# Keys and queries loaded in runs of six tokens, and put in order by products that write their columns six apart

## The chip, the cores and the metric

The kernel runs on one core of one Trainium2 chip. The metric is the device time in microseconds (us) of one execution, and the lower the better. A core has a matrix engine (TensorE, PE in the profile; its loading of weights is the row PEld), VectorE (DVE), ScalarE (ACT), GpSimd (POOL) and SyncE (SP, which here issues all transfers). The matrix engine reads SBUF and writes PSUM.

## The reference, cut to what matters

An attention feeds two mixtures of experts. The attention has 4 batches of 8 heads, 576 tokens and 64 features; it is the sum of a coarse part over the means of four tokens and of a local part over the seven nearest tokens.

```python
q_d = q.reshape(B, H, Sd, factor, D).mean(axis=3)      # factor = 4, Sd = 144; k_d, v_d alike
out_up = np.repeat(sm_attn(q_d, k_d, v_d), factor, axis=2)
mask = np.abs(pos[:, None] - pos[None, :]) < factor
scores = np.where(mask, scale * np.matmul(q, k.transpose(0, 1, 3, 2)), -1000000000.0)
...
x = (out_up + softmax(scores) @ v)                     # as [2304 tokens, 512 features]
x = _moe_ref(x, phi, w1, w2)                           # first mixture, 8 experts of 4 slots
return _moe2_ref(x, w_gate, w1, w2)                    # second mixture, 8 experts of 1024
```

## The kernel before, in words

The attention goes by units: a unit is a pair of heads of one batch, so there are 16 units, four to a batch. Each unit passes through some 35 parts (load, transpose, copy, score, softmax, products, sum), and the table ORDER writes down by hand in which order a step emits its parts and by how many steps each lags behind. A step therefore holds one part of each kind, for different units, and each engine runs its own parts in that order. Four batch parts (lps; lt and lnp; dnp; sip) join in three of each four steps.

The parts that the change touches are these. `load_qk` (L193) asks for keys and queries, one step before they are used. Keys come with tokens 96 i to 96 i + 95 side by side on 96 partitions, one run of 64 features (256 bytes) for each token and head. Queries come in the same way, but for the units in WIDE_Q (0, 2, 3, 9, 12, 13): there each partition takes six tokens that follow each other, one run of 1,536 bytes. `transpose_k` (L238) and `transpose_q` (L262) put the features on the partitions, in PSUM tiles kps and qps: six transposes of 96 columns, or for the queries of WIDE_Q twelve products with the identity, each of a head's 64 features. In the second form token 6 g + i lands at place g of product i, so `copy_q` (L277) puts the tokens in order on its way from PSUM to SBUF:

```python
out=t[:, 0:S].rearrange("p (g a i) -> p a i g", a=2, i=3),
in_=pv.rearrange("p a (i g) -> p a i g", i=3), func=ACTF.Copy,
```

`pool_k` (L247, tile kd) on VectorE and `copy_k` (L253, tile kt) on ScalarE read kps; `copy_q` (tile qt) reads qps; the scores `score_loc` (L313, tile sl) and `score_pool` (L327, tile sd) follow. kps, qps, ptp, loc, lps and lt share two buffers in PSUM (the pool p2, tag t2).

SP issues the transfers in the order of the steps: keys and queries of one unit, weight tiles (wa, 1 MB each) where LOADS asks for some, then the values twice, as windows (vw, runs of 256 bytes) and as groups of four tokens (vg, runs of 1,024 bytes). After the loop SP asks for the other 24 weight tiles. Then comes the first mixture (its first product is tile h at L711) and the second, which takes the larger part of the time and is TensorE's.

Of the kernel before, what the change touches and what calls it, by code (L numbers as in the profile page):

```python
# [18 lines left out]
# A step of the attention, in order of emission: a part, and by how many steps it lags behind the  # L19
# unit's (or, for the parts in BATCH, the batch's) own step.  # L20
# [11 lines left out]
# What the steps leave of the last units and batches, in order of emission.  # L32
# [9 lines left out]
# Weight tiles of the first mixture that are asked for in a step.  # L42
LOADS = {-2: 1, 8: 2, 9: 1, 11: 2, 12: 2, 15: 3}
# Units before this one keep their pooled queries padded with zero rows, the others a head at a time.
PADDED = 2
# Units whose queries come in long runs and are transposed by products with the identity.
WIDE_Q = frozenset((0, 2, 3, 9, 12, 13,))
# [3 lines left out]
def attn_moe_moe_kernel(  # L51
# [13 lines left out]
    nc = tc.nc  # L65
# [39 lines left out]
    def make_masks(m0):  # L105
        # keys 1 .. 7 after the query's place in its block; the first and the last block also
        # lose the keys that pass the ends of the sequence
# [60 lines left out]
    # =================== attention ===================  # L168
    with ExitStack() as actx:
# [19 lines left out]
        def rows(src, b, h, first, ap):  # L189
            s0 = src[b, h]  # L190
            return bass.AP(tensor=s0.tensor, offset=s0.offset + first * D, ap=ap)

        def load_qk(u):  # L193
            b, hp = units[u]
            d = U[u] = {}
            kn = d["kn"] = lq.tile([96, 6, 2, D], FP32, name="kn", tag="kn")
            for h in range(2):
                nc.sync.dma_start(
                    out=kn[:, :, h, :], in_=k[b, 2 * hp + h].rearrange("(i g) d -> g i d", i=6)
                )  # L200
            if u in WIDE_Q:
                qn = d["qn"] = lq.tile([96, 2, 6 * D], FP32, name="qn", tag="qn")
                nc.sync.dma_start(out=qn, in_=rows(q, b, 2 * hp, 0, [[6 * D, 96], [S * D, 2], [1, 6 * D]]))
            else:
                qn = d["qn"] = lq.tile([96, 6, 2, D], FP32, name="qn", tag="qn")
                for h in range(2):
                    nc.sync.dma_start(
                        out=qn[:, :, h, :], in_=q[b, 2 * hp + h].rearrange("(i g) d -> g i d", i=6)
                    )

        def load_v(u):
            # vw: the keys of window t = 4 s + c (24 t - 4 .. 24 t + 28) on partitions 32 c ..;
            # what a window holds past the ends of its sequence has weight zero
# [23 lines left out]
        # q and k with the features of both heads on the partitions  # L237
        def transpose_k(u):  # L238
            d = U[u]
            ps = d["kps"] = p2.tile([128, 2, 512], FP32, name="kps", tag="t2")  # L240
            for i in range(6):
                nc.tensor.transpose(  # L242
                    ps[:, i // 3, 96 * (i % 3):96 * (i % 3) + 96],
                    d["kn"][:, i].rearrange("p h d -> p (h d)"), ident[0:96, 0:96],
                )
# [7 lines left out]
        def copy_k(u):  # L253
            # the keys of a head keep the rows of the other head zero
# [7 lines left out]
        def transpose_q(u):  # L262
            d = U[u]
            qn = d["qn"]
            ps = d["qps"] = p2.tile([128, 2, 512], FP32, name="qps", tag="t2")
            for i in range(6):
                ov = ps[:, i // 3, 96 * (i % 3):96 * (i % 3) + 96]
                if u in WIDE_Q:
                    for h in range(2):
                        nc.tensor.matmul(  # L270
                            out=ov[64 * h:64 * h + 64, :], lhsT=qn[:, h, D * i:D * i + D],
                            rhs=ident[0:96, 0:96], start=True, stop=True,
                        )
                else:
                    nc.tensor.transpose(ov, qn[:, i].rearrange("p h d -> p (h d)"), ident[0:96, 0:96])

        def copy_q(u):  # L277
            t = U[u]["qnt"] = qts[u % 2]
            pv = U[u]["qps"][:, :, 0:288]
            if u in WIDE_Q:  # L280
                # token 6 g + i of a head stands at place g of product i
                nc.scalar.activation(
                    out=t[:, 0:S].rearrange("p (g a i) -> p a i g", a=2, i=3),
                    in_=pv.rearrange("p a (i g) -> p a i g", i=3), func=ACTF.Copy,
                )
            else:
                nc.scalar.activation(out=t[:, 0:S].rearrange("p (a j) -> p a j", a=2), in_=pv, func=ACTF.Copy)

        def pool_q(u):
# [7 lines left out]
            if u < PADDED:  # L297
                # the queries of a head keep the rows of the other head zero
# [191 lines left out]
        # tokens of a batch on the partitions: four tiles, and the last 64 on the upper half  # L490
# [560 lines left out]
```

## Time and profile before

| | |
|---|---|
| Time, median of 3 runs | 1129.81 us (1126.55 to 1130.12) |
| Span of the profiled execution | 1131.3 us; no other time is recorded with it |
| TensorE busy | 1084.3 us, 96% of the span |
| VectorE busy | 523.4 us, 46% |
| ScalarE busy | 361.8 us, 32% |
| First product of the first mixture starts | 171.88 us after the span's start |
| Packets of all transfers | 95,887, 93.41 MB |

The shares are means over the whole span; the attention is only its first 170 us, so it is read from windows of that stretch. Matrix products are pipelined, so that the time of a group of them is better read from its first start to the start of the next group than from its busy time. An fp32 product appears as two instructions (passes), a transpose as one.

### The profile page before, as it was taken

Reading aid. Unit: us, or ns where it says so; the run is one execution under the profiler, and the core shown is the slowest. Engines: PE = TensorE matmul, PEld = TensorE weight load, DVE = VectorE, ACT = ScalarE, POOL = GpSimd, SP = SyncE. Lnnn points to the kernel's source line nnn. Section 1 sums busy time; section 2 is a strip of 40 time slices with the busy share of each in tenths; the row PEclk is TensorE's granted clock in tenths of the full one; section 3 lists DMA queues with packets and bytes.
Section 4 is the critical chain, followed back from the end, with each engine's and each line's share of the span. In section 5 each row is a group of like instructions: output and inputs, shape, how many; then the busy total and the mean of one; then the engine's idle time right before and its main releaser. Section 6 shows DMA issues by size and latency. Waiting matters only on the chain.

```text
span 1131.3 us, 16288 instructions
## 1 busy us (share of the span) xinstructions
PE 1084.3 (96%) x6639; PEld 854.9 (76%) x6639; DVE 523.4 (46%) x1161; ACT 361.8 (32%) x946; POOL 214.5 (19%) x178
## 2 busy tenths in 40 slices
PE   6788877999999999999999999999999999999998
PEld 5666643387888788878887888788788878888886
DVE  5996963165544434344334333434343344334332
ACT  5886741143222322232223222322232222222221
POOL 5654431060049100400040004000400040000000
PEclk9998988889999999999999999999999999999999
DMA  9999998942002200220022002200220010001011
GB/s 193 168 202 214 246 389 313 387 149 75 1 1 75 75 1 1 75 75 1 1 75 75 1 1 75 75 1 1 75 75 1 1 38 1 1 1 38 38 47 47
DMA packets 95887, 93.41 MB, mean 83 GB/s; under 512 B 59076, under 2 KB 64836, under 8 KB 95812
## 3 DMA queue, kind: packets, MB, share of 16 engines
q1 hardware_dynamic: 95812, 92.37, 29.3%
q8 instruction: 52, 0.85, 0.3%
q14 instruction: 23, 0.19, 0.1%
HBM read 87.64 MB, written 4.72 MB: 82 GB/s over the span
## 4 chain that ended last, share of the span: by engine, by line
PE 84%; DVE 1%; ACT 0%; issue 0%; DVEq 0%
PE y L875 71%; PE h L857 6%; PE h L711 1%; PE ap L828 1%; PE so L760 1%; PE as L840 1%; PE sip L610 0%; PE hps L749 0%; DVE c L738 0%; PE cp L734 0%; ACT c L736 0%; PE sp L939 0%; PE sit L691 0%; PE gl L908 0%; ACT aps L832 0%
## 5 line engine op out<-in xcount | busy, mean ns | idle before, releaser
L861 DVE SCALAR_TENSOR_TENSOR hlo<-h,hhi 128x256 fp32r<-128x256 f32 x576 | 243.9, 424 | 499.9 <-ACT hhi L860 498.9
L875 PE MATMUL y<-whi,hlo 128*128 128x512 f32 x1152 | 457.2, 397 | 0.0
L875 PE MATMUL y<-whi,hhi 128*128 128x512 f32 x1152 | 456.9, 397 | 0.0
L875 PE MATMUL y<-wlo,hhi 128*128 128x512 f32 x1152 | 454.6, 395 | 0.0
L860 ACT ACTIVATE hhi<-h 128x256 fp32r<-128x256 f32 x576 | 221.3, 385 | 632.0 <-PE h L857 632.0
L875 PEld LDWEIGHTS y<-whi,hhi 128*128 128x128 f32 x1152 | 216.5, 188 | 57.9 <-ACT aps L832 5.9
L875 PEld LDWEIGHTS y<-wlo,hhi 128*128 128x128 f32 x1152 | 216.8, 188 | 48.5
L875 PEld LDWEIGHTS y<-whi,hlo 128*128 128x128 f32 x1152 | 218.5, 190 | 25.8
L857 PE MATMUL h<-c,a4s 128*128 128x256 f32 x576 | 161.8, 282 | 0.0
L857 PEld LDWEIGHTS h<-c,a4s 128*128 128x128 f32 x576 | 108.9, 189 | 28.5 <-DVE a4s L845 1.7
L810 POOL CAST whi<-w2s 128x2048 fp32r<-128x2048 f32 x14 | 26.5, 1895 | 483.5 <-PE y L875 474.8
L884 DVE SCALAR_TENSOR_TENSOR acc<-y,pg,acc 128x512 f32<-128x512 f32 x126 | 93.7, 743 | 9.9 <-PE y L875 9.7
L811 POOL TENSOR_TENSOR wlo<-w2s,whi 128x2048 fp32r<-128x2048 f32 x14 | 64.7, 4620 | 1.1
L892 POOL TENSOR_SCALAR acc<-acc,pg 128x512 f32<-128x512 f32 x18 | 27.8, 1564 | 79.3 <-DVE pg L949 79.3
L405 DVE STREAM_TRANSPOSE bd<-pl 32x384 f32<-32x384 f32 x64 | 36.4, 569 | 1.9 <-POOL pl L391 0.5
L242 PE MATMUL kps<-ident,kn 96*128 96x96 f32 x96 | 13.1, 282 | 17.5 <-DMA kn<-in_k_dram 9.3
L242 PEld LDWEIGHTS kps<-ident,kn 96*128 96x128 f32 x96 | 10.1, 161 | 21.5 <-issue 9.4
L257 ACT ACTIVATE kt<-kps 64x576 f32<-64x576 f32 x32 | 20.5, 642 | 12.6 <-DVE kd L249 12.4
L391 POOL TENSOR_TENSOR pl<-pl,l 128x384 f32<-128x384 f32 x16 | 13.3, 831 | 57.2 <-DVE l L387 54.5
L400 ACT ACTIVATE pd<-pd,ls 72x144 f32<-72x144 f32 x64 | 21.3, 406 | 8.7 <-DVE ls L386 7.6
L374 ACT ACTIVATE pd<-sd,nm 72x144 f32<-72x144 f32 x64 | 23.1, 372 | 0.1
L464 PE MATMUL loc<-bd,vw 128*64 128x96 f32 x384 | 20.7, 261 | 2.0 <-ACT dT L581 1.6
(169 smaller groups left out, 669.9 us busy)
## 6 DMA issues: line engine op xcount, KB each, us to landing
wa<-in_moe_w_dram SPq DMA_DIRECT2D x32, 1024.0 KB, 7.6
w1s<-in_moe_w_dram SPq DMA_DIRECT2D x16, 1024.0 KB
w2s<-in_moe_w_dram SPq DMA_DIRECT2D x15, 1024.0 KB, 6.9
vw<-in_v_dram SPq DMA_DIRECT2D x62, 96.0 KB, 6.2
kn<-in_k_dram SPq DMA_DIRECT2D x32, 144.0 KB, 6.0
vg<-in_v_dram SPq DMA_DIRECT2D x16, 288.0 KB
out_dram<-acc SPq DMA_DIRECT2D x18, 256.0 KB, 2.0
qn<-in_q_dram SPq DMA_DIRECT2D x20, 144.0 KB, 5.9
```

The lines of the kernel that those rows point to most:

```text
L242: nc.tensor.transpose(ps[:, i // 3, 96 * (i % 3):96 * (i % 3) + 96], d["kn"][:, i].rearrange("p h d -> p (h d)"), ident[0:96, 0:96],)
L374: nc.scalar.activation(out=pd[:, h, a, :], in_=d["sdv"][:, h, a, :], func=ACTF.Exp, scale=scale / 16.0, bias=d["nm"][:, h, a:a + 1], accum ...
L400: nc.scalar.activation(out=d["pd"][:, h, a, :], in_=d["pd"][:, h, a, :], func=ACTF.Copy, scale=ls[:, h, a:a + 1])
L405: nc.vector.transpose(out=bds[u % 2][32 * c:32 * c + 32, :, c, :], in_=U[u]["pl"][32 * c:32 * c + 32])
L810: nc.gpsimd.tensor_copy(out=hi, in_=t)
L811: nc.gpsimd.tensor_tensor(out=lo, in0=t, in1=hi.bitcast(FP32), op=ALU.subtract)
L857: nc.tensor.matmul(out=ps, lhsT=a4s[:, e % 2, 128 * f:128 * f + 128], rhs=c4[:, BLK * b:BLK * b + BLK], start=True, stop=True)
L860: nc.scalar.activation(out=hi[:, f, :], in_=ps, func=ACTF.Relu)
L861: nc.vector.scalar_tensor_tensor(out=lo[:, f, :], in0=ps, scalar=0.0, in1=hi[:, f, :].bitcast(FP32), op0=ALU.max, op1=ALU.subtract)
L875: nc.tensor.matmul(out=ps, lhsT=l[:, f, ts], rhs=r, start=(n == 0), stop=(n == 3 * KF - 1))
L884: nc.vector.scalar_tensor_tensor(out=acc[:, t, :], in0=ps, scalar=pg[:, t, e:e + 1], in1=acc[:, t, :], op0=ALU.mult, op1=ALU.add)
L892: nc.gpsimd.tensor_scalar(out=acc[:, t, :], in0=acc[:, t, :], scalar1=pg[:, t, 0:1], scalar2=None, op0=ALU.mult)
```

## The change

All keys and queries, of every unit, come in the form with six tokens a partition: two transfers for the keys and two for the queries, each of 48 partitions (0 to 47 and 64 to 111, one half of the tokens each) with runs of 1,536 bytes. Both transpositions are made by products with the identity, 24 of them: six token places i, two heads h, two halves a. Each reads 48 partitions, has 64 output partitions and 48 columns, and writes these columns six apart in PSUM, so that token 6 g + i stands at place 6 g + i. `copy_q` has one form left, and WIDE_Q is gone.

```diff
-            kn = d["kn"] = lq.tile([96, 6, 2, D], FP32, name="kn", tag="kn")
-            for h in range(2):
-                nc.sync.dma_start(
-                    out=kn[:, :, h, :], in_=k[b, 2 * hp + h].rearrange("(i g) d -> g i d", i=6)
-                )
...
+            for name, src in (("kn", k), ("qn", q)):
+                t = d[name] = lq.tile([112, 2, 6, D], FP32, name=name, tag=name)
+                for a in range(2):
                     nc.sync.dma_start(
-                        out=qn[:, :, h, :], in_=q[b, 2 * hp + h].rearrange("(i g) d -> g i d", i=6)
+                        out=t[64 * a:64 * a + 48].rearrange("p h i d -> p h (i d)"),
+                        in_=rows(src, b, 2 * hp, 288 * a, [[6 * D, 48], [S * D, 2], [1, 6 * D]]),
                     )
...
+        def transpose(t, ps):
+
+            for i in range(6):
+                for h in range(2):
+                    for a in range(2):
+                        r = slice(64 * a, 64 * a + 48)
+                        nc.tensor.matmul(
+                            out=ps[64 * h:64 * h + 64, a, 0:288].rearrange("p (g i) -> p i g", i=6)[:, i, :],
+                            lhsT=t[r, h, i, :], rhs=ident[r, r], start=True, stop=True,
+                        )
+
         def transpose_k(u):
-            d = U[u]
-            ps = d["kps"] = p2.tile([128, 2, 512], FP32, name="kps", tag="t2")
-            for i in range(6):
-                nc.tensor.transpose(
-                    ps[:, i // 3, 96 * (i % 3):96 * (i % 3) + 96],
-                    d["kn"][:, i].rearrange("p h d -> p (h d)"), ident[0:96, 0:96],
-                )
+            ps = U[u]["kps"] = p2.tile([128, 2, 512], FP32, name="kps", tag="t2")
+            transpose(U[u]["kn"], ps)
...
         def copy_q(u):
             t = U[u]["qnt"] = qts[u % 2]
             pv = U[u]["qps"][:, :, 0:288]
-            if u in WIDE_Q:
...
+            nc.scalar.activation(out=t[:, 0:S].rearrange("p (a j) -> p a j", a=2), in_=pv, func=ACTF.Copy)
```

TensorE's order in a plain step of the loop, before (a row is a group of like instructions, with the output's partitions and columns; numbers behind a name tell buffers apart):

```order
L242 MATMUL kps<-ident,kn 128x96 x6
L445 MATMUL up<-ptd,vd 64x144 x4
L464 MATMUL loc<-bd_120,vw 64x96 x12
L497 MATMUL xn<-ident,xt_116 128x128 x4
L498 MATMUL xh<-ident,xt_116 128x128
L275 MATMUL qps<-ident,qn 128x96 x6
L425 MATMUL ptp<-ident,pd 72x72 x8
L320 MATMUL sl<-kt_110,qt_108 32x64 x24
L333 MATMUL sd<-kd,qd_112 72x144 x4
```

The same step with the change:

```order
L238 MATMUL kps<-ident,kn 64x48 x24
L427 MATMUL up<-ptd,vd 64x144 x4
L446 MATMUL loc<-bd_120,vw 64x96 x12
L479 MATMUL xn<-ident,xt_116 128x128 x4
L480 MATMUL xh<-ident,xt_116 128x128
L238 MATMUL qps<-ident,qn 64x48 x24
L407 MATMUL ptp<-ident,pd 72x72 x8
L302 MATMUL sl<-kt_110,qt_108 32x64 x24
L315 MATMUL sd<-kd,qd_112 72x144 x4
```

The order is the same; six transposes have become 24 smaller products, once for the keys and once for the queries.

SP's order where two steps ask for weights, before (the shape is that of the tile's side; the first qn is of a unit outside WIDE_Q, the second of one inside):

```order
L198 DMA kn<-in_k_dram 96x6x64 x2
L207 DMA qn<-in_q_dram 96x6x64 x2
L162 DMA wa<-in_moe_w_dram 128x2x1024 x2
L221 DMA vw<-in_v_dram 32x12x64 x4
L231 DMA vg<-in_v_dram 72x4x256
L198 DMA kn<-in_k_dram 96x6x64 x2
L203 DMA qn<-in_q_dram 96x2x384
L162 DMA wa<-in_moe_w_dram 128x2x1024
```

And with the change:

```order
L200 DMA kn<-in_k_dram 48x2x384 x2
L200 DMA qn<-in_q_dram 48x2x384 x2
L161 DMA wa<-in_moe_w_dram 128x2x1024 x2
L215 DMA vw<-in_v_dram 32x12x64 x4
L225 DMA vg<-in_v_dram 72x4x256
L200 DMA kn<-in_k_dram 48x2x384 x2
L200 DMA qn<-in_q_dram 48x2x384 x2
L161 DMA wa<-in_moe_w_dram 128x2x1024
```

The queue keeps its order; the runs of kn and qn are 384 elements long instead of 64, and a unit of WIDE_Q has two transfers of qn in place of one.

## Rows read from the trace of the kernel before

**Rows 1.** TensorE's timeline: start, duration, instructions; the first mixture's first product.

```profile
171.88 16.80 PE L711 MATMUL h<-wa,slt 128*32 128x512 f32 x128 [0.44 <-DVE slt L703]
```

**Rows 2.** TensorE's timeline, transpositions of keys; in brackets the idle time before.

```profile
22.74 0.69 PE L242 MATMUL kps<-ident,kn 96*128 96x96 f32 x6 [0.60 <-DMA kn<-in_k_dram]
...
29.20 0.69 PE L242 MATMUL kps<-ident,kn 96*128 96x96 f32 x6 [0.71 <-DMA kn<-in_k_dram]
...
36.60 0.69 PE L242 MATMUL kps<-ident,kn 96*128 96x96 f32 x6 [1.36 <-ACT pd L400]
...
43.90 0.69 PE L242 MATMUL kps<-ident,kn 96*128 96x96 f32 x6 [0.99 <-ACT pd L400]
...
52.52 0.69 PE L242 MATMUL kps<-ident,kn 96*128 96x96 f32 x6 [2.31 <-DMA kn<-in_k_dram]
...
59.56 0.69 PE L242 MATMUL kps<-ident,kn 96*128 96x96 f32 x6 [0.72 <-DMA kn<-in_k_dram]
...
67.82 0.69 PE L242 MATMUL kps<-ident,kn 96*128 96x96 f32 x6 [0.29 <-ACT pd L400]
...
76.34 0.71 PE L242 MATMUL kps<-ident,kn 96*128 96x96 f32 x6
...
85.46 0.71 PE L242 MATMUL kps<-ident,kn 96*128 96x96 f32 x6
...
94.64 0.69 PE L242 MATMUL kps<-ident,kn 96*128 96x96 f32 x6 [2.73 <-DMA kn<-in_k_dram]
...
105.83 1.18 PE L242 MATMUL kps<-ident,kn 96*128 96x96 f32 x6 [2.24 <-DMA kn<-in_k_dram]
...
117.43 0.72 PE L242 MATMUL kps<-ident,kn 96*128 96x96 f32 x6
...
127.01 0.72 PE L242 MATMUL kps<-ident,kn 96*128 96x96 f32 x6
```

**Rows 3.** Windows: stretch, length, each engine's busy time, granted clock, DMA share, GB/s.

```profile
70.00:80.00 10.00, 9.95 (x160) 8.10 (x156) 9.62 (x23) 9.25 (x25) 5.66 (x8) 1.00 1.18 182
100.00:110.00 10.00, 7.76 (x128) 6.10 (x124) 5.31 (x14) 6.29 (x19) 4.65 (x6) 0.79 1.15 183
145.00:150.00 5.00, 3.39 (x52) 2.98 (x51) 4.61 (x16) 2.96 (x11) 0.74 (x2) 1.00 1.02 406
```

**Rows 4.** TensorE's timeline, other groups of the steps from 36.60 and 52.52.

```profile
40.40 0.69 PE L425 MATMUL ptp<-ident,pd 72*72 72x72 f32 x8 [0.17 <-DVE xt L474]
...
42.20 0.71 PE L333 MATMUL sd<-kd,qd 64*72 64x144 f32 x8 [0.30 <-ACT pd L374]
...
57.32 0.88 PE L320 MATMUL sl<-kt,qt 128*32 128x64 f32 x48
58.13 0.71 PE L333 MATMUL sd<-kd,qd 64*72 64x144 f32 x8
...
60.18 0.71 PE L445 MATMUL up<-ptd,vd 72*64 72x144 f32 x8
```

**Rows 5.** Waits of the whole span: who waited for whom, total, times, longest.

```profile
PE kps L242 <- DMA kn<-in_k_dram: 9.3, 6, 2.7
```

**Rows 6.** The page's count of packets.

```profile
DMA packets 95887, 93.41 MB, mean 83 GB/s; under 512 B 59076, under 2 KB 64836, under 8 KB 95812
```

**Rows 7.** TensorE's timeline, queries of a unit in WIDE_Q and what follows.

```profile
99.19 1.21 PE L270 MATMUL qps<-ident,qn 96*64 96x96 f32 x24
100.33 0.69 PE L425 MATMUL ptp<-ident,pd 72*72 72x72 f32 x8
```

**Rows 8.** TensorE's timeline, the first scores of the opening.

```profile
11.68 1.51 PE L320 MATMUL sl<-kt,qt 128*32 128x64 f32 x48
```

**Rows 9.** The tile qps: ScalarE's copies, ns min/median/max, first and last start.

```profile
L287 ACT ACTIVATE qt<-qps x10: 646/651/655, 12.5 to 132.4; 128x576 f32<-128x576 f32 x10
L282 ACT ACTIVATE qt<-qps x6: 1193/1203/1233, 9.3 to 115.5; 128x576 f32<-128x576 f32 x6
```

More of the change, by code (lines that the diff above doesn't have):

```diff
@@ L45 @@
 PADDED = 2
-WIDE_Q = frozenset((0, 2, 3, 9, 12, 13,))
 @with_exitstack
@@ L195, in load_qk @@
             d = U[u] = {}
-            kn = d["kn"] = lq.tile([96, 6, 2, D], FP32, name="kn", tag="kn")
-            for h in range(2):
-                nc.sync.dma_start(
-                    out=kn[:, :, h, :], in_=k[b, 2 * hp + h].rearrange("(i g) d -> g i d", i=6)
-                )
-            if u in WIDE_Q:
[L202 to L206, printed above, removed]
+            for name, src in (("kn", k), ("qn", q)):
+                t = d[name] = lq.tile([112, 2, 6, D], FP32, name=name, tag=name)
+                for a in range(2):
                     nc.sync.dma_start(
-                        out=qn[:, :, h, :], in_=q[b, 2 * hp + h].rearrange("(i g) d -> g i d", i=6)
+                        out=t[64 * a:64 * a + 48].rearrange("p h i d -> p h (i d)"),
+                        in_=rows(src, b, 2 * hp, 288 * a, [[6 * D, 48], [S * D, 2], [1, 6 * D]]),
                     )
@@ L262, in transpose_q @@
         def transpose_q(u):
[L263 to L275, printed above, removed]
+            ps = U[u]["qps"] = p2.tile([128, 2, 512], FP32, name="qps", tag="t2")
+            transpose(U[u]["qn"], ps)
         def copy_q(u):
@@ L279, in copy_q @@
             pv = U[u]["qps"][:, :, 0:288]
[L280 to L287, printed above, removed]
+            nc.scalar.activation(out=t[:, 0:S].rearrange("p (a j) -> p a j", a=2), in_=pv, func=ACTF.Copy)
         def pool_q(u):
```

## Prediction

> **What bounds the kernel now.** I read the windows first, then TensorE's timeline, then the waits. Behind the attention nothing in the change reaches: the first mixture's first product starts at 171.88 us [rows 1], and from there TensorE works in the order it has today. So the question is when the attention ends, and what paces its steps.
>
> A step has one transposition of keys (kps) and one of queries (qps) on TensorE, so the starts of kps [rows 2] give the length of each step. Four kinds of step come round in each batch of four units: a plain one, one with the logits (lps), one with lt and lnp, one with dnp and sip. First round: 36.60 to 43.90 is a plain step, 7.30 us; 59.56 to 67.82 (lps) 8.26; 67.82 to 76.34 (lt, lnp) 8.52; 76.34 to 85.46 (dnp, sip) 9.12. None of these four ends in a wait for a transfer. In them the engines are nearly full: from 70 to 80 us TensorE is busy 9.95 of 10 us, VectorE 9.62, ScalarE 9.25 [rows 3]. The plain step still holds 0.17 + 0.30 + 0.99 us of TensorE idle [rows 2, 4], the others next to none.
>
> Other steps of the same kinds are longer: 43.90 to 52.52 takes 8.62 us, 85.46 to 94.64 9.18, 94.64 to 105.83 11.19, 105.83 to 117.43 11.60, 117.43 to 127.01 9.58. Three of them end in waits of 2.31, 2.73 and 2.24 us for the transfer of kn [rows 2], and all six waits of kps for that transfer sum to 9.3 us [rows 5]. The DMA engines are at a share above 1 throughout while they move only 182 or 183 GB/s; once only weights are in flight, at the same full share, they move 406 [rows 3]. The short runs are what fills them: 59,076 of 95,887 packets are below 512 bytes [rows 6]. [...]
>
> **What the change removes.** Against its own kind each starved step is too long by 1.32 (8.62 - 7.30), 1.88 (9.18 - 7.30), 2.93 (11.19 - 8.26), 3.08 (11.60 - 8.52) and 0.46 us (9.58 - 9.12): 9.7 us in all. That goes if the keys arrive in time. Do they? From 70 to 80 us a unit with short queries moves 1.28 MB (576 KB of keys and queries, 384 of vw, 288 of vg, in units of 1024 bytes); at 182 GB/s that is 7.0 us. Its vg comes in runs of 1 KB; at the 406 GB/s of the weights it would take 0.73. That leaves 6.3 us for 0.98 MB in 256-byte runs, 157 GB/s, and 3.75 us of them for keys and queries. In runs of 1,536 bytes, at the weights' rate, these take 1.45 us: an estimate of 4.7 us for a unit, well inside the shortest step. A step that also asks for two weight tiles needs 4.7 + 2.1 MB / 406 GB/s = 9.9 us, about 1 us more than it has. I give back 1.0 us for that.
>
> Before the first full round kps waits 0.60 and 0.71 us for its transfer (22.74 and 29.20) [rows 2], 1.3 us more. The 0.72 at 59.56 I leave out: the step that it ends took 7.04 us, less than a plain one.
>
> **What it adds: TensorE's products.** A transposition of keys is now 6 instructions, start to next start 0.62 us (59.56 to 60.18) [rows 2, 4]; of short queries the same; of wide queries 24 passes over 12 products, 1.14 us (99.19 to 100.33) [rows 7]. The new form is 24 products, 48 passes, of 48 columns each, for both. No row writes columns six apart, and none uses quarters of the array as 64 by 64. Bounds: the scores sl are also 48 passes, with four groups of output partitions in turn, 0.81 us (57.32 to 58.13) [rows 4]; no row is cheaper for so many. The wide queries cost 47.5 ns a pass with two groups; 48 such passes are 2.28 us, the upper end. If the columns alone counted, half of that, 1.14. I take 0.81. Four groups (two heads, two halves of the keys) alternate as in sl, and two halves of the rows do overlap in sd: 8 passes of 144 columns in 0.71 us, 89 ns each [rows 4], where the wide queries' 47.5 ns for 96 columns scale to 71 at twofold overlap; a pass alone would be near double that.
>
> So keys cost 0.19 us more, short queries 0.19, wide queries 0.33 less. Of the six steps in which TensorE is full, three carry wide queries (units 9, 12, 13): 3 x 0.38 - 3 x 0.14 = 0.7 us. In six plain or early steps VectorE's kd comes 0.19 later: 1.1. Together 1.8 us. In the opening TensorE runs at its lower clock: sl takes 1.51 us there against 0.88 [rows 4, 8], 1.7 times as long. By that factor three transpositions of keys and one of queries become longer by 0.3 each, two of wide queries shorter by 0.6: nothing in sum.
>
> **What costs nothing.** ScalarE's copies of wide queries fall from 1.20 us to 0.65, six times [rows 9]. The cover is TensorE's own work, ptp, sl and sd, between qps and the next kps; without that cover 3.3 us would be gained. SP issues four transfers for keys and queries where it issued three or four, one more in six units. The queue has the same transfers behind them, vw and the weights, and these come sooner, not later. No part is moved on any engine. After the loop the weights' transfers start sooner by what the loop gains, so the rest shifts as one piece; late next would be VectorE and ScalarE, at 9.62 and 9.25 of 10.
>
> **Sum.** -9.7 - 1.3 + 1.0 + 1.8 = -8.2 us. The profiled execution spans 1131.3, 1.5 above the median of the runs; taken off the median of 1129.8 this gives 1121.6, rounded to 1122 us. Its own range is 1116 to 1127. What a measurement here can tell from no change is 0.3%, 3.4 us.
>
> **Rivals.**
> *The products overlap less, TensorE becomes the bound (slower).* At 1.7 us a transposition, the middle of 1.14 and 2.28, keys and short queries cost 2.16 us more a step, with wide queries 1.64. The full steps grow by 3 x 2.16 + 3 x 1.64 = 11.4; six plain steps go from 7.30 to 5.84 + 0.47 + 2.16 = 8.47, another 7.0; the opening, at twice the price and about half covered, 5. Against 10.0 saved (9.7 + 1.3 - 1.0) that is +13: 1143. At 2.28 it would be near 1160. It decides from about 1.2 us a transposition, where added and saved are equal. For it speaks that the wide queries, with 64 output partitions, show nothing like sl's 17 ns a pass; against it, that they have two groups in turn, not four. Chance 0.16.
>
> *The columns six apart cost more than columns side by side.* Then the four groups overlap, but each column counts like two: 24 ns a pass, 1.14 us, up to 1.4. Full steps grow by 4.7 to 7.8, kd in six others comes 3.1 to 4.7 later, the opening takes 1.5 to 2.5 more, against 10.0 saved: 1129 to 1135, about no change. No row speaks for or against. [...] Chance 0.16.
>
> *The waits for transfers do not go, only shrink.* The weights and vw stay in the queue ahead of the keys, and in the long steps from 85.46 on weights are asked for. If only the step without weights before it (43.90) and a third of the others heal, 1.3 + 2.8 + 1.3 - 1.8 = 3.6 us: 1126. Chance 0.12.
>
> The forecast has 0.56. Range 1114 to 1141: below lies a gain also from the shorter copies, above the price of 1.7 us and more. Faster by over 0.3%: most of the forecast and half of the last rival, with a little of the second, 0.60; within: 0.17; slower: 0.23.
>
> **What would show it.** Right: no wait of kps for kn above 0.5 us; TensorE's granted clock at 1.00 from 90 to 120 us; kps and qps 0.8 to 0.9 us start to start; plain steps of 7.3 to 7.6; the first product of the mixture at about 164 instead of 171.88 us. Wrong: kps above 1.2 us, VectorE waiting for kps in each step, TensorE at 9.9 of 10 in plain steps; or waits for kn of 2 us that remain.

## The result: slower, 1144.48 us

The changed kernel takes 1144.48 us (median, 1137.71 to 1148.35) against 1130.58 of the kernel before on the same chip: ratio 1.0109, 95% interval 1.0076 to 1.0141. The forecast was 1122, its range 1114 to 1141. The first product of the first mixture starts at 186.26 us instead of 171.88 [rows 1], 14.4 later; the span grows by 12.4. So the loss lies in the attention, as the gain was meant to.

The page of the changed kernel: the span with all instructions, TensorE's row, the packets, the queue that carries instructions (transfers, MB, share of the engines).

```profile
span 1143.7 us, 18755 instructions
...
PE 1100.1 (96%) x7875; PEld 869.9 (76%) x7875; DVE 524.8 (46%) x1161; ACT 359.3 (31%) x946; POOL 214.8 (19%) x178
...
DMA packets 71033, 93.57 MB, mean 82 GB/s; under 512 B 29220, under 2 KB 39972, under 8 KB 70948
...
q8 instruction: 62, 1.02, 0.4%
```

The short packets halve [rows 6], and between 20 and 150 us kps waits for kn not once, where it waited 9.3 us [rows 5]. What came instead stands in TensorE's timeline of the changed kernel (start, duration, and in brackets the idle time before it and its releaser; passes behind the x):

```profile
95.52 0.38 PE L407 MATMUL ptp<-ident,pd 72*72 72x72 f32 x3 [0.22 <-DVE xt L456]
97.95 0.81 PE L407 MATMUL ptp<-ident,pd 72*72 72x72 f32 x5 [2.05 <-issue]
98.69 1.51 PE L302 MATMUL sl<-kt,qt 128*32 128x64 f32 x48
...
101.30 0.92 PE L238 MATMUL kps<-ident,kn 48*64 48x48 f32 x48
102.15 0.71 PE L427 MATMUL up<-ptd,vd 72*64 72x144 f32 x8
102.69 0.58 PE L446 MATMUL loc<-bd,vw 128*64 128x96 f32 x9
105.33 1.54 PE L446 MATMUL loc<-bd,vw 128*64 128x96 f32 x15 [2.06 <-issue]
```

The products themselves cost what was forecast: kps, 48 passes, takes 0.85 us from its start to that of up (forecast 0.81). But TensorE stops in the midst of ptp after 3 of its 8 passes, and of loc after 9 of 24, for 2.05 and 2.06 us, and "issue" says that nothing in the trace releases it. All passes of such a group have the same operands, and for the pass behind the stop the profile shows nothing that it waited for, so no transfer of data and no other engine stands there as what is late. Behind the first stop sl runs at the lower clock (1.51 us, at the higher 0.88 [rows 4]; the granted clock is 0.50 from 98.70 to 100.10 us, and 1.00 from 55 to 60), behind the second loc (0.50 from 105.40 to 106.80). The granted clock by windows of the changed kernel (the third number from the end; a number between these two levels I read as a mean of them):

```profile
20.00:30.00 10.00, 6.40 (x173) 5.52 (x166) 5.46 (x14) 6.62 (x19) 4.65 (x6) 0.64 1.11 167
30.00:40.00 10.00, 10.00 (x197) 8.85 (x198) 8.08 (x18) 7.81 (x28) 4.65 (x6) 0.51 0.69 123
100.00:110.00 10.00, 7.94 (x153) 6.55 (x146) 7.03 (x12) 4.76 (x17) 3.81 (x5) 0.67 0.87 158
```

Where in the loop the time goes is read from the start of the n-th kps, against [rows 2]: the sixth 41.78 (5.2 us later than before), the tenth 72.15 (4.3), the thirteenth 101.30 (6.7), the fourteenth 115.16 (9.3), the fifteenth 124.11 (6.7), the sixteenth 139.11 (12.1). What is lost up to the sixth is lost behind two more stops, of 2.10 us at 15.22 us and of 0.67 us at 21.19 us.

**Where the stops stand.** The passes between two stops can be counted, here from the one at 54.74 to the one at 64.41:

```profile
54.74 0.65 PE L302 MATMUL sl<-kt,qt 128*32 128x64 f32 x32 [0.50 <-issue]
55.33 0.71 PE L315 MATMUL sd<-kd,qd 64*72 64x144 f32 x8
55.97 0.91 PE L238 MATMUL kps<-ident,kn 48*64 48x48 f32 x48
56.82 0.71 PE L427 MATMUL up<-ptd,vd 72*64 72x144 f32 x8
57.36 1.16 PE L446 MATMUL loc<-bd,vw 128*64 128x96 f32 x24
58.45 0.66 PE L479 MATMUL xn<-ident,xt 128*128 128x128 f32 x4
58.94 0.27 PE L480 MATMUL xh<-ident,xt 128*128 128x128 f32 x1
60.43 0.91 PE L238 MATMUL qps<-ident,qn 48*64 48x48 f32 x48 [1.22 <-ACT pl L348]
61.28 0.69 PE L407 MATMUL ptp<-ident,pd 72*72 72x72 f32 x8
61.90 0.88 PE L302 MATMUL sl<-kt,qt 128*32 128x64 f32 x48
62.71 0.71 PE L315 MATMUL sd<-kd,qd 64*72 64x144 f32 x8
63.35 0.44 PE L238 MATMUL kps<-ident,kn 48*64 48x48 f32 x15
64.41 0.72 PE L238 MATMUL kps<-ident,kn 48*64 48x48 f32 x33 [0.61 <-issue]
```

That is 32 + 8 + 48 + 8 + 24 + 4 + 1 = 125 passes to the pause ahead of qps, and 48 + 8 + 48 + 8 + 15 = 127 from there. Counted each time from the stop before, 252 passes lie ahead of the stop at 73.99, 505 ahead of 97.95, 126 ahead of 105.33 and 379 ahead of 125.53: multiples of 126, within one. A pass is two instructions (product and load of weights; the page counts 7,875 of each), so it is a count of some 252 instructions. The page has 2,467 instructions more than before, and its instruction queue 10 transfers more (52 before): 247 instructions each. In the windows 95.0 to 95.2 and 102.4 to 102.6 us of the changed kernel, the view of the DMA queues has these rows of that queue

```profile
q8 instruction: 1, 0.02, 42.5%
...
q8 instruction: 1, 0.02, 41.7%
```

and for 95.2 to 102.4 it has no row of that queue. So a block's transfer stands at 95.1 and the next at 102.5, 2.8 or 2.9 us before TensorE goes on; for 54.74, 60.43, 64.41 and 69.59 it stands at 51.9, 57.5, 61.7 and 66.8, 2.7 to 2.9 us before. From 20 to 133 us these transfers come every 6 to 12 us in before (8.7 on average), in the changed kernel every 4 to 9 (5.9). If the transfers belong to the ends of blocks in the same order in both kernels, then in before each stands 4.9 us or more ahead of the time at which TensorE gets there, and none is late.

Three pauses of the changed kernel stand at such places but bear the name of a releaser: 1.22 us at 60.43, 0.67 us at 69.59, and the longest of the loop, 126 passes behind the stop at 125.53:

```profile
132.96 1.51 PE L302 MATMUL sl<-kt,qt 128*32 128x64 f32 x48 [2.25 <-DVE xb L490]
```

sl does not read xb, and in before it does not wait at this place (123.04 us). The run with 30 passes put ahead, below, shows that these pauses too go with the count. With them the pauses at ends of blocks sum to 13.3 us; "issue" alone gives 9.2. The step from the fifteenth kps to the sixteenth, which holds two of them (0.88 and 2.25 us) and the lower clock behind the second (0.50 from 133.0 to 134.4 us), takes 15.0 us instead of 9.6.

So the theory for the experiments: **TensorE runs out of instructions.** They come in blocks by DMA (62 transfers of the instruction queue), a block lasts 126 passes by the places of the stops, and the change makes a step of 113 passes one of 197, of short passes. Rivals: the columns six apart, the shapes of the products, the transfers.

### The profile page after: what moved, and what is told of

Read it like the earlier page. It is cut to its first block, busy times and chain, and to the rows that moved or that the text cites. A ratio compares the mean times of both kernels' runs of the same rounds, so it can differ in the third digit from the quotient of the medians.

```text
span 1143.7 us, 18755 instructions
## 1 busy us (share of the span) xinstructions
PE 1100.1 (96%) x7875; PEld 869.9 (76%) x7875; DVE 524.8 (46%) x1161; ACT 359.3 (31%) x946; POOL 214.8 (19%) x178
## 3 DMA queue, kind: packets, MB, share of 16 engines
q8 instruction: 62, 1.02, 0.4%
## 4 chain that ended last, share of the span: by engine, by line
PE 83%; DVE 1%; ACT 0%; issue 0%; DVEq 0%
PE y L857 71%; PE h L839 6%; PE so L742 1%; PE h L693 1%; PE ap L810 1%; PE as L822 1%; PE hps L731 0%; DVE c L720 0%; PE cp L716 0%; PE sip L592 0%; ACT c L718 0%; PE sp L921 0%; DVE aps L815 0%; ACT aps L814 0%; PE sop L752 0%
## 5 line engine op out<-in xcount | busy, mean ns | idle before, releaser
L238 PE MATMUL kps<-ident,kn 48*64 48x48 f32 x768 | 19.5, 253 | 7.5 <-DMA kn<-in_k_dram 5.1
L238 PEld LDWEIGHTS kps<-ident,kn 48*64 48x64 f32 x768 | 16.8, 166 | 12.5 <-issue 8.9
L373 POOL TENSOR_TENSOR pl<-pl,l 128x384 f32<-128x384 f32 x16 | 13.3, 831 | 64.1 <-DVE l L369 60.6
L302 PE MATMUL sl<-kt,qt 128*32 128x64 f32 x768 | 18.1, 250 | 6.3 <-issue 3.3
L446 PEld LDWEIGHTS loc<-bd,vw 128*64 128x64 f32 x384 | 20.8, 157 | 4.4 <-issue 2.2
```

The costliest lines, as they stand in the source:

```text
L238: nc.tensor.matmul(out=ps[64 * h:64 * h + 64, a, 0:288].rearrange("p (g i) -> p i g", i=6)[:, i, :], lhsT=t[r, h, i, :], rhs=ident[r, r], ...
L446: nc.tensor.matmul(out=loc[64 * h:64 * h + 64, s // 3, 96 * (s % 3):96 * (s % 3) + 96], lhsT=d["vw"][:, NSET * h + s, :], rhs=bd[:, 2 * s ...
```

## Experiments

The runs on whose times and stops the argument rests are in one table; the other four (e2, e3, e6, e14) stand with their ratios where they are told. Passes are those of a transposition of keys; blocks are the transfers of the instruction queue; stops are TensorE's pauses of 0.25 us and more up to 165 us with "issue" as releaser (those ahead of sd aside, which stand at its first pass in nearly every run, the longest of them 2.00 us in the change and 0.67 in before); kn is the wait of kps for its transfer between 20 and 150 us; h is the mixture's first product. Stops, kn and h are of one execution each: two of the same kernel, e1 and e15, have h at 174.56 and 167.46, so the ratio decides. With the pauses at ends of blocks that bear another name the sums of stops are 13.3 us for the change, 11.3 for e4, 3.1 for e7, 8.9 for e11 and 7.0 for e13; e5 and e10 have none of these.

| run | passes | blocks | stops, us | kn, us | h | ratio, 95% interval |
|---|---|---|---|---|---|---|
| before | 6 | 52 | 0 | 9.3 | 171.88 | 1 |
| the change | 48 | 62 | 8, 9.2 | 0 | 186.26 | 1.0109 (1.0076 to 1.0141) |
| e1_loads_only | 6 | 51 | 1, 0.4 | 6.0 | 174.56 | 1.0013 (0.9992 to 1.0035) |
| e15_loads_again | 6 | 51 | 0 | 5.4 | 167.46 | one execution |
| e4_side_by_side | 48 | 62 | 6, 9.0 | 0 | 180.68 | 1.0105 (1.0067 to 1.0143) |
| e5_shift30 | 48 | 62 | 8, 9.9 | 0 | 183.91 | one execution |
| e7_after_late | 48 | 62 | 3, 1.5 | 0 | 169.35 | 1.0102 (1.0057 to 1.0148) |
| e9_twelve | 12 | 53 | 0 | 0 | 168.93 | 0.9959 (0.9931 to 0.9988) |
| e10_half | 24 | 56 | 2, 2.4 | 2.1 | 166.68 | 0.9961 (0.9931 to 0.9991) |
| e13_half_count | 48 | 62 | 6, 5.8 | 0 | 184.54 | 1.0102 (1.0052 to 1.0151) |
| e8_before_spread | 6 | 52 | 0 | 12.5 | 179.97 | 1.0088 (1.0057 to 1.0119) |
| e11_after_end | 48 | 62 | 8, 7.3 | 0 | 176.90 | 1.0033 (1.0011 to 1.0055) |
| e12_before_end | 6 | 52 | 0 | 5.1 | 169.51 | 0.9966 (0.9940 to 0.9992) |

### The parts of the change

**The loads alone**, six transposes as before:

```diff
-                t = d[name] = lq.tile([112, 2, 6, D], FP32, name=name, tag=name)
+                t = d[name] = lq.tile([96, 2, 6, D], FP32, name=name, tag=name)
...
+                nc.tensor.transpose(
+                    ps[:, i // 3, 96 * (i % 3):96 * (i % 3) + 96], w[:, 128 * i:128 * i + 128], ident[0:96, 0:96]
+                )
```

> The transfers of the change, with the six transposes of before for keys and queries (each reads 128 neighbouring features of the longer rows, so the features of the attention are mixed up; copies as in the change). Theory A (TensorE's instructions arrive in blocks of 126 matmuls with their weight loads, and it runs dry where a block is used up sooner than the next arrives): the number of instructions is back to that of before, so no pauses inside groups of more than 0.7 us; the waits for kn go, granted clock 1.00 from 60 to 140 us; 1119 to 1123 us, the gain that the prediction gave to the transfers. Theory B (the columns written six apart, or the quarters of the array, make the loss): the same, 1119 to 1123. Theory C (the transfers were never worth it, the waits only move to another cause): 1127 to 1132.

No gain: 1.0013. Its waits (TensorE's, 20 to 150 us: sum, times, longest) and the place of the longest:

```profile
PE kps L236 <- DMA kn<-in_k_dram: 6.0, 3, 4.8
...
95.31 1.19 PE L236 MATMUL kps<-ident,kn 96*128 96x96 f32 x6 [4.83 <-DMA kn<-in_k_dram]
```

The gain of theories A and B (1119 to 1123 us) did not come; the median is 1133.98 us. Long runs did not take the waits away here. A second execution shows that they stay, in other places:

> The change's loads with six transposes, on partitions 0 to 95, once more (features mixed, as there), for one look: is its wait of kps for kn of 4.83 us at 95.31 us a matter of this arrangement or of one execution? If of the arrangement: again a wait of 3.5 us or more for kn between 85 and 120 us, and waits of kn of 5 us or more in sum from 30 us on. If of one execution: under 2 us in sum, as with 12 transposes on partitions 0 to 47 and 64 to 111.

2.36 us at 93.05 and 1.80 at 103.03, 5.4 in sum: the two executions agree in the sum and not in the single long wait.

**The products alone (the first line), and more products on the loads alone (the others).**

```diff
+                        r, c = slice(64 * a, 64 * a + 48 - 16 * a), slice(64 * a, 64 * a + 48)
...
+                for c in range(4 if i % 2 else 3):
+                    nc.tensor.matmul(
+                        out=ps[32 * c:32 * c + 32, i // 3, 400:402], lhsT=w[:, 128 * i:128 * i + 32],
+                        rhs=ident[0:96, 0:2], start=True, stop=True,
+                    )
```

> The transfers of before, with the 24 products of the change for every transposition, columns six apart (each reads 48 or 32 partitions of the old rows, so keys and queries are mixed up; copies as before). Theory A: pauses every 126 matmuls as with the change, and more of them or longer, since the transfers fill the DMA engines as before, waits for kn besides: 1145 to 1165 us. A theory by price alone (0.84 us a transposition, as the change shows it, and nothing else): 1132 to 1135, before plus the 1.8 us of the prediction.

> As the first of these runs, with 21 small products of two columns added to each transposition, which write PSUM columns that nobody reads, side by side: 48 matmuls a transposition as in the change, with none six apart and no quarters of the array. Theory A: the pauses come back every 126 matmuls; 1138 to 1150 us. Theory B: no pauses inside groups; a longer transposition (some 1.2 us) alone, 1122 to 1130.

Ratios 1.2209 (1.2149 to 1.2269) and 1.0637 (1.0600 to 1.0675). The pauses that the theory of the count gave for both did not come: with 62 blocks, as in the change, neither has a stop. But a transposition itself became dear, so a block lasts longer, 12 to 21 us in the first and 6 to 11 in the second (20 to 200 us). In both, shapes alternate, and I take that for the cause. In the first, 48 and 32 rows in turn:

```profile
51.26 9.03 PE L243 MATMUL qps<-ident,qn 48*64 48x48 f32 x48
```

That is 9.03 us for 48 passes at the lower clock (0.50 from 50 to 60 us), where those of the change take 1.46 at the same 0.50 (139.11 us). In the second a transposition takes 2.41 us (105.92 us). Both are inconclusive.

**Columns side by side:**

```diff
-    out=ps[64 * h:64 * h + 64, a, 0:288].rearrange("p (g i) -> p i g", i=6)[:, i, :],
+    out=ps[64 * h:64 * h + 64, a, 48 * i:48 * i + 48],
```

> The change with the 48 columns of each product side by side in PSUM in place of six apart (the tokens then stand out of order). Theory A: nothing changes, kps 0.84 us from start to next start, pauses every 126 matmuls, 1138 to 1148 us. Theory B (six apart is what costs): 1120 to 1125, kps below 0.84, no pauses.

```profile
100.98 0.92 PE L238 MATMUL kps<-ident,kn 48*64 48x48 f32 x48
101.83 0.71 PE L427 MATMUL up<-ptd,vd 72*64 72x144 f32 x8
...
106.35 1.55 PE L446 MATMUL loc<-bd,vw 128*64 128x96 f32 x15 [3.40 <-issue]
```

0.85 us, as six apart, the same stop in loc after 9 passes, the same time. The columns six apart cost nothing that shows.

### Is it the count of instructions?

**The same program, 30 passes later in the count:**

```diff
+            for _ in range(15 if u == 0 else 0):
+                nc.tensor.matmul(
+                    out=ps[0:64, 0, 400:402], lhsT=ident[0:48, 0:64], rhs=ident[0:48, 0:2], start=True, stop=True
+                )
```

> Added: 15 products of two columns (30 passes) ahead of the first transposition of the keys; their result is read by nobody. Theory (TensorE's instructions come in blocks, and a block's end is a place in the count of its instructions, whatever work stands there): every pause of TensorE that nothing in the trace releases moves 30 passes earlier in the program. In the changed kernel these pauses stand after 3 passes of ptp (97.95 us), after 9 of loc (105.33), after 20 of kps (125.53), after 16 of sl (54.74) and after 15 of kps (64.41); now they stand 30 passes ahead of these places, in qps ahead of ptp, in kps ahead of loc, in the last passes of the sl ahead of kps, and so on, and none is left in the old places. Time 1138 to 1149 us. Rival (the pause belongs to the work there: a write to PSUM, a wait that the trace does not show): the pauses stay in ptp, loc, kps and sl at the same pass.

In the changed kernel, then in this one:

```profile
53.81 0.43 PE L302 MATMUL sl<-kt,qt 128*32 128x64 f32 x16
54.74 0.65 PE L302 MATMUL sl<-kt,qt 128*32 128x64 f32 x32 [0.50 <-issue]
```

```profile
49.92 0.90 PE L238 MATMUL qps<-ident,qn 48*64 48x48 f32 x42 [0.69 <-ACT kt L261]
51.38 0.33 PE L238 MATMUL qps<-ident,qn 48*64 48x48 f32 x6 [0.56 <-issue]
...
65.92 0.56 PE L238 MATMUL qps<-ident,qn 48*64 48x48 f32 x22 [0.79 <-issue]
...
89.09 0.24 PE L306 MATMUL sl<-kt,qt 128*32 128x64 f32 x1 [2.30 <-issue]
```

The stop in sl after 16 passes went to qps after 42 (48 + 8 + 16 - 30 = 42, exact). The first one, in sl after 30, went to just ahead of the same sl (14.47, 2.44 us); the one in kps after 20 to sl after 47 (expected 46; 0.41 us); the one in kps after 15 to sl after 42 (expected 41; 0.20 us). The pause ahead of sl at 69.59, which bore the name of ACT pd, went to qps after 26 (48 + 8 - 30, exact) and has lost that name. None is left in the old places, those of the three named pauses included. Those expected in qps (after 21) and in kps (after 35) are gone, and a longer one stands a block or two sooner, at 89.09: the count says where a stop can be, not how long it is. The rival, that a stop belongs to the work, falls.

**As many empty instructions in the kernel before:**

```diff
+                for _ in range(14):
+                    nc.tensor.nop()
```

> The kernel before, with its loads and its transposes, and with as many empty instructions on TensorE as the change adds in its passes: 14 ahead of each of the six transposes of the keys, 14 ahead of each of the six of short queries, 8 ahead of each of the six places of wide queries (84 to 168 a step; 2,400 in all). No product and no transfer is changed. [...] Rival (products of 48 rows and columns, or the loads with 64 + 48 partitions, cause the pauses): no pauses, time 1128 to 1134 us.

1.0006 (0.9979 to 1.0033), but void: the trace holds 16,288 instructions and 52 blocks, as before. So the empty instructions never reached TensorE, and nothing was added.

**Half the products, and the count restored.**

```diff
-            for i in range(6):
+            for i in range(0, 6, 2):
...
-                            lhsT=t[r, h, i, :], rhs=ident[r, r],
+                            lhsT=t[r, h, i, :], rhs=ident[r, r].unsqueeze(1).to_broadcast([48, 2, 48]),
```

> The changed kernel, but a product writes the columns of two token places at once (96 columns): 12 products, 24 passes a transposition, the same columns in all, the same six places apart, the same shapes of rows and output partitions, the same transfers. What is left out: every second token is a copy of the one before it. Theory (the count of instructions): half of the added passes go, about 150 passes a step instead of 197; the pauses are fewer, the last up comes between 135 and 143 us, and the time is 1130 to 1140 us, between before and the change. Rival (the columns, the shapes or the transfers cost it): kps stays at 0.85 us and the time at 1140 to 1149 us.

```profile
q8 instruction: 56, 0.92, 0.4%
...
91.17 0.73 PE L238 MATMUL kps<-ident,kn 48*64 48x96 f32 x24
91.82 0.71 PE L427 MATMUL up<-ptd,vd 72*64 72x144 f32 x8
...
99.03 0.64 PE L302 MATMUL sl<-kt,qt 128*32 128x64 f32 x13 [1.29 <-issue]
...
166.68 15.71 PE L693 MATMUL h<-wa,slt 128*32 128x512 f32 x128 [0.44 <-DVE slt L685]
```

Ratio 0.9961, better than expected: with the same transfers, rows, output partitions and columns, half the passes turn the loss into a gain. kps takes 0.65 us. From here to the change lie 1.5%, 17 us; the dearer transposition is 0.20 us, 32 times, 6.4 us if every one lay on the path. The rest I put down to the stops and the lower clock behind them (mean granted clock 0.980 here, 0.967 in the change).

```diff
+                        nc.tensor.matmul(
+                            out=ps[64 * h:64 * h + 64, a, 400:402],
+                            lhsT=t[r, h, i + 1, :], rhs=ident[r, 64 * a:64 * a + 2], start=True, stop=True,
+                        )
```

> The run with 12 products of 96 columns a transposition (every second token a copy of the one before it, as there), and behind each product one of two columns that nobody reads: 48 passes a transposition again, as in the changed kernel, with hardly any columns more. Theory (the count of instructions is what costs): the pauses come back at the changed kernel's places in the count, after 222, 1106 and 1358 passes from the start and at further multiples of 126; 62 blocks of instructions instead of 56; the time is 1137 to 1148 us, ratio to before 1.005 to 1.014. Rival (the number of products that write PSUM six apart, or their columns, cost it; the small products hide behind them): no new pauses in the loop, time as with half the products, 1125 to 1132 us.

```profile
q8 instruction: 62, 1.02, 0.4%
...
89.89 0.34 PE L238 MATMUL qps<-ident,qn 48*64 48x96 f32 x4 [1.75 <-issue]
...
103.66 0.51 PE L411 MATMUL ptp<-ident,pd 72*72 72x72 f32 x5 [0.70 <-issue]
...
108.47 0.88 PE L450 MATMUL loc<-bd,vw 128*64 128x96 f32 x15 [0.80 <-issue]
```

1.0102. The stops are back, in ptp after 3 and in loc after 9 passes as in the change, 254 and 126 passes apart; of the three places named beforehand one (1106) shows a stop. The run is not clean as to time: a transposition here takes 1.00 us from start to start, 0.35 more than with half, which by itself could be up to 11 us.

**Twelve passes:**

```diff
+                    nc.tensor.transpose(ps[:, a, 48 * i:48 * i + 48], w[r, 128 * i:128 * i + 128], ident[r, r])
```

> The changed kernel's transfers exactly (halves on partitions 0 to 47 and 64 to 111), with 12 transposes of 48 rows and 128 columns in place of the 24 products: 12 passes a transposition instead of 48. What is left out: a transpose takes two tokens of one head instead of one token of two heads, so features and heads are mixed and the output is not the reference's. Theory (the transfers with halves at 0 and 64 do free the DMA engines, and the 48 passes throw the gain away): waits of kps for kn in the loop (20 to 150 us) sum to under 3 us, as in the changed kernel, pauses without a releaser come seldom and the last up is at 127 to 133 us; time 1120 to 1129 us. Rival (the loads bring nothing in themselves; the waits for kn of 4.83 us as in the run with six transposes stay): 1130 to 1136 us.

0.9959: no stop, no wait for kn in the loop. **A step between** did not test what it was made for:

```diff
+                        if h == 0:
+                            nc.tensor.transpose(out, t[r, h, i, :], ident[r, r])
```

> The changed kernel with the first head's products made transposes (one pass for 48 columns instead of two): 36 passes a transposition; the same transfers, columns and places, and the reference's output. Theory (the time follows the count): 173 passes a step, between 149 (half the products, ratio 0.996) and 197 (the change, 1.011); 59 blocks of instructions; ratio 1.000 to 1.007. Rival (a threshold: anything above half brings the pauses fully): 1.008 to 1.014.

1.0544 (1.0507 to 1.0581): transposes and products in turn take 3.60 us a transposition in one place (57.40 to the next group at 61.00, TensorE busy without a gap) and 2.47 in another (103.33 to 105.80). With 59 blocks there is no stop, but a block lasts 6 to 14 us here. So it says nothing of the count.

### What the DMA engines have to do with it

**No early weight tiles in the changed kernel:**

```diff
-LOADS = {-2: 1, 8: 2, 9: 1, 11: 2, 12: 2, 15: 3}
+LOADS = {15: 3}
```

> The changed kernel, with no weight tile asked for in the loop before its last step (three there, as before; eight fewer in all), so that keys, queries and values have the DMA engines for themselves. Theory (blocks of instructions come over the same DMA engines as the data, and a pause is as long as the queues are full): the pauses of 2.05 and 2.06 us at 97.95 and 105.33 shrink to 1.2 us or less, the granted clock of 100 to 130 us is above 0.9, and the last up comes at 140 to 145 us instead of 148.15; the first mixture waits for its weights later, so that the end is at 1135 to 1150 us. Rival (a pause does not hang on the load of the DMA engines): the pauses are as long as in the changed kernel, 2 us each, and the loop ends at 147 to 149 us.

The places of the 2-us stops, here without one, and the mixture:

```profile
97.80 0.69 PE L407 MATMUL ptp<-ident,pd 72*72 72x72 f32 x8
...
102.72 1.21 PE L446 MATMUL loc<-bd,vw 128*64 128x96 f32 x24
...
169.35 15.49 PE L693 MATMUL h<-wa,slt 128*32 128x512 f32 x128 [0.44 <-DVE slt L685]
...
214.36 1.93 PE L742 MATMUL so<-wa,hT 128*32 128x512 f32 x8 [1.65 <-DMA wa<-in_moe_w_dram]
```

With the same 62 blocks the stops shrink from 9.2 to 1.5 us, and h starts 17 us sooner than in the change, 2.5 sooner than before. Then the first mixture waits for its weights (so, 1.65 us and others), and the time ends at 1.0102. From 40 to 95 us, where the change asks for tiles only from 80.6 us on, the pauses at ends of blocks are alike, 3.3 us in the change and 3.1 here (1.56 of them at 55.38 us, with the name of ACT pd); what is gone are those in the opening and from 95 us on, all of 2 us and more among them. So the count makes the places, and the length goes with the transfers beside them, here eight weight tiles of 1 MB fewer in the loop. Whether a block's transfer waits for anything there, the trace does not show.

**Early tiles moved behind the last keys and queries**, in the changed kernel and in the one before, and **spread, one a step**, in the one before:

```diff
+LOADS = {-2: 1, 13: 3, 14: 3, 15: 4}
...
+LOADS = {-2: 1, 4: 1, 5: 1, 6: 1, 7: 1, 8: 1, 9: 1, 10: 1, 15: 3}
```

> The changed kernel with seven of its early weight tiles asked for in steps 13 and 14 and in the last step (3, 3 and 4), behind the last keys and queries, instead of steps 8 to 12 and 15. Theory (a pause is long where transfers fill the DMA engines): the loop is as in the run without early tiles, last up at 125 to 131 us, with two or three pauses of about 1 us in the steps with tiles; the first mixture's first product at 166 to 174 us and its weights in time for most of it: 1122 to 1134 us. Rival (what the tiles cost in one place they cost in another): 1137 to 1146 us.

> The kernel before with the same places for the early weight tiles. Theory (weights in the queue make the keys late, not their short runs alone): the waits of kps for kn at 94 to 117 us vanish, under 2 us in sum from 30 us on; the last up comes at 125 to 130 us instead of 133.66; time 1120 to 1130 us. Rival (short runs alone make the keys late): waits of 2 us and more stay in steps without a tile, the last up at 131 to 135 us; time 1128 to 1136 us.

> The kernel before with the same eight early weight tiles asked for one a step, in steps 4 to 10, instead of two in steps 8, 11 and 12 and one in step 9. Theory (keys are late because two tiles and vw stand ahead of them in the queue, not because of their short runs): the waits of kps for kn of 2.2 to 2.7 us at 94 to 117 us go below 1 us each, from 9.3 us in all to 5 or less, and the last up comes 2 to 5 us sooner than 133.66; the time is 1124 to 1130 us. Rival (short runs are what makes keys late): the waits move to the steps with the tiles and sum to 9 us or more; time 1130 to 1136 us.

TensorE's waits of the moved and of the spread version of before, 20 to 150 us:

```profile
PE kps L242 <- DMA kn<-in_k_dram: 5.1, 6, 1.7
```

```profile
PE kps L242 <- DMA kn<-in_k_dram: 12.5, 7, 4.8
```

Moved, the waits fall from 9.3 to 5.1 us (the largest 1.67; forecast under 2 in all), and of the versions that leave nothing of the work out this is the one that beats both kernels: 0.9966 of before, 1130.46 us against 1133.79 of before. Spread, they rise to 12.5 and the time to 1.0088: my theory there, that pairs of tiles are what hurts, fell; single tiles between the keys hurt more. The changed kernel with moved tiles, 1.0033, gains 0.8% on the change and stays behind before: 1137.43 us, at the rival's lower bound and not in the 1122 to 1134 of the theory.

## Why the prediction was wrong, step by step

- **That the attention's end decides, and no later stage:** right; 14.4 of the mixture's start reach the end as 12.4.
- **"What the change removes", 9.7 + 1.3 - 1.0 = 10.0 us:** the mechanism holds in part. The waits for kn do go, to 0 in the change. But with few passes (e9, e10) the whole gain is 0.4%, 4.5 us, less than half; with six transposes (e1) it is none. The 4.7 us worked out for a unit's transfers was too low: in 60 to 80 us of e10 the DMA engines have a share of 0.90 to 0.91 at one unit a step of 8.4 and 8.5 us, where 4.7 would give 0.56. The share above 1 in before did not mean what I read: it stays at 1.02 to 1.15 in e1 from 30 to 90 us, with long runs of keys and queries (vw still comes in runs of 256 bytes). The 3.08 us of the step from 105.83 I counted in because the granted clock of before is 0.79 from 100 to 110 us [rows 3], 0.50 from 105.9 to 106.9, behind the wait of 2.24 us; the change has 0.67 from 100 to 110 us, without a wait for kn.
- **"What it adds", 0.81 us a transposition:** right, 0.85; the first rival's price (1.2 and more) and the second's (columns six apart) did not come. That a column six apart counts like two, no run shows: side by side (e4) it is 0.85 as well.
- **"What costs nothing": this is the step that failed.** I priced products by their time on the array alone, and put their number at nothing without a reason. A product is also two passes and four instructions (384 products of keys are 768 matmuls and 768 loads of weights in the trace of the change); 42 more passes for keys, as many for short queries, 24 for wide ones. That opened a wait that no term, bound or rival held: 9.2 us of stops, 13.3 with the three that bear another name, and the lower clock behind the long ones. The opening, costed at nothing, lost 5.2 us by the sixth kps, with stops of 2.10 and 0.67 us and the clock at 0.51 from 30 to 40 us; e7, with the same products and neither stop, has its sixth kps 1.1 us sooner than before. The lower clock that I named for the opening of before is not in its granted clock: sl takes 1.51 us there [rows 8] with 1.00 from 11.70 to 13.10 us.
- **That the clock would be at 1.00 from 90 to 120 us:** it was at 0.89, 0.67 and 0.75 in the three windows of 10 us, and with this clock goes most of what TensorE is busy longer. Before and then the change, from the span's start to the mixture's first product (TensorE's busy time is the number behind the first comma, the clock the third from the end):

```profile
0.00:171.88 171.88, 136.50 (x2105) 103.92 (x2105) 129.90 (x304) 113.68 (x320) 85.81 (x124) 0.95 1.09 237
...
0.00:186.26 186.26, 154.90 (x3341) 120.07 (x3341) 131.26 (x304) 111.12 (x320) 85.76 (x124) 0.85 0.87 217
```

  TensorE is idle 31.4 us in the change and 35.4 in before: in the sum of idle time the stops only took the place of other waits, those for kn among them. It is busy 18.4 us longer. By the times above the dearer transpositions are 4.2 us of that, an estimate for the higher clock (0.23 for 16 of keys and 10 of queries, less 0.29 for the 6 of wide queries); the rest, some 14 us, I put down to work at the lower clock.
- **The rival of 1143 us** named about the right time by luck: its reason, a transposition of 1.7 us, was not there.
- **The signs of a wrong prediction that I listed**, a kps above 1.2 us at the higher clock and waits for kn that remain, were not what showed. TensorE is full in some stretches (10.00 of 10 from 30 to 40 us), but at a clock of 0.51, not from dear products.

That the stops are instructions arriving late is inferred, from four things that agree: their places (the count, shifted by 30 when 30 passes were put ahead), the transfers some 2.8 us ahead of them, fewer with fewer passes, shorter with less other traffic. Still open: why the loads alone bring nothing with six transposes on partitions 0 to 95 and 0.4% with 12 or 24 passes and the second half at partition 64; the two differ in both.

## What to carry to other kernels

Count instructions as well as time. Where an edit turns few large operations into many small ones, divide the engine's passes in a step by the passes between two stops (126 here) and ask whether the next block arrives in time under the load of the step's transfers. The sign of it here was a pause in the midst of a group of equal operations, released by "issue", 126 passes or a multiple of that behind the last one, and the test was to shift the stream by 30 passes. Here weight tiles asked for between the loads of a pipelined loop cost more than tiles asked for behind the last of them (in before, 1.0088 spread and 0.9966 moved). And look at the granted clock as well as at the stops: up to the mixture TensorE's idle time did not grow here (31.4 us, 35.4 in before), its busy time did (154.9, 136.5 in before).

## What the hardware showed that was not expected

TensorE stops for up to 3.40 us at ends of blocks of 126 passes (the loc of e4), and the transfer of a block stands 2.3 to 3.2 us before TensorE goes on (in the change, from 130.6 to 132.96 and from 70.8 to 73.99 us). The 2 x 7,875 instructions of TensorE on the page of the change come to 254 for each of its 62 transfers, the 2 x 6,639 on that of before to 255 for each of 52. In before no stop of 0.25 us and more with "issue" as releaser stands in the loop, those ahead of sd aside; in the change there are eight up to 165 us, of 0.3 to 2.1 us, 9.2 in sum. Columns 24 bytes apart cost nothing here, 0.85 us for 48 passes either way. And groups in which shapes alternate were dear: 48 and 32 rows, 9.03 us for 48 passes at the lower clock (e2, 51.26 us); transposes and products of the same 48 rows, 2.47 us for 36 passes (e14, 103.33 us).
